# An opening in a pinned order: the short chunk's bias first, its stores and first reads ahead of loads of V, later K and weights

## The chip, the cores and the metric

The kernel runs on one core of one Trainium2 chip, as one program. The core has TensorE (PE in the profile), VectorE (DVE), ScalarE (ACT), GpSimd (POOL) and SyncE (SP, which here only issues transfers), and 16 DMA engines that move data between HBM and on-chip memory. The metric is the time of one execution in device microseconds, the median of several runs.

## The reference

Attention for 4 batch rows, 8 heads, 576 positions and head size 64, with a bias that a small network computes from the distance of two positions, followed by a feed-forward layer with a squared ReLU over 2304 tokens. Cut to what is computed:

```python
scores = (1 / sqrt(D)) * q @ k.T                       # 4 x 8 x 576 x 576
x = log1p(abs(i - j)) / log1p(max(i, 1))               # 576 x 576
bias = relu(x[..., None] @ w1 + b1) @ w2               # hidden size 32, one bias per head
attn = softmax(scores + bias); y = attn @ v            # 2304 x 512 after heads are joined
out = relu(y @ w_in) ** 2 @ w_out                      # 512 -> 2048 -> 512
```

## The kernel before

**Work.** The batch rows are taken in two pairs p, and each pair in five chunks c of queries: chunk 0 is the short one (the last 64 positions of both rows of the pair, in one tile of 128 rows), chunks 1 to 4 are 128 positions. A step is one (p, c, head); there are 80 steps, chunk by chunk in the order of ORDER, chunk 0 of pair 0 first. In a step, `qk` (L359) makes the scores on PE, `softmax_a` (L386) adds the bias tile `bt` and takes the row maximum on DVE (L398, the instruction by which the start of a step is told below) and exponentiates on ACT, `softmax_b` transposes, and three steps later `pv` multiplies with V. When the eight heads of a chunk are done, `finish_x` passes the chunk to the expert layer, which is worked through in eight units of 256 hidden columns (`g1`, tile `hp`, L522; `g2`, L545) between the steps. Most operands are split into two fp16 parts, so each weight block of 512 KB that is loaded costs three DVE operations of 512 columns (`WT.split`, L206, L207, L209), an ACT cast and two POOL operations. The 32 blocks are loaded (`ld_dma`) through three buffers and split (`ld_split`) by a list W_AT, three, then two a step.

**Bias.** The bias depends on two positions and a head only. It is computed once, in 36 groups of 16 positions, of which the four groups 32 to 35 belong to the short chunk and come first. For each group `hgen` (L268) makes four tiles of the hidden layer, on ACT or DVE by a pattern (`PATS[HID[...]]`, where A is ACT and D is DVE: "AADD" makes two on each). `bias_mm` (L303) multiplies them with `w2s` on PE in two pieces per group (288 columns and the rest), each into a PSUM tile `bp`, evicts each piece (L332 on ACT, L334 on DVE) into a tile `be` and stores it to the table `biasd` in HBM (L337). The first piece of a group has two evictions on ACT, the second one on DVE. `bias_ld` (L341) reads the table back, skewed, into the tile `bt` that a step adds: two loads of 144 KB for the short chunk, three buffers. The first step's loads must wait for all eight stores of the short chunk.

**Order.** The program is written as below; a planner then gives each engine and each DMA queue one fixed order, from the order of the text and its own estimate of when each instruction becomes ready. All plain transfers here go through SP's queue, which issues in order: an issue that waits holds up those behind it. Because a load of V or K needs only a free buffer, the planner could put it ahead of a store that was not ready. K of step t is loaded to one of two staging buffers (L162) and split by POOL (`kv_split`); V has nine buffers.

The lines that set the opening before:

```python
    nc.sync.dma_start(out=tab_t, in_=tabs)
    nc.sync.dma_start(out=sm_t, in_=sm)
    kv_dma(0)
    ...
    while gi < bias_due(-1):
        hgen(groups[gi], ("hg", "a", "at", "s")[gi % 4])
        bias_mm(groups[gi], gi)
        gi += 1
```

Of the kernel before, what the change touches and what calls it, by code (L numbers as in the profile page):

```python
# [2 lines left out]

# [5 lines left out]
F32 = mybir.dt.float32  # L9
# [4 lines left out]
ALU = mybir.AluOpType  # L14
# [19 lines left out]
}  # L34

PATS = ["DDDD", "ADDD", "AADD"]
HID = "222222222211111000"

W_AT = [3, 2, 2, 2, 2, 2, 2, 2, 2, 2, 2, 2, 2, 2, 2, 1]
ORDER = [[0, 3, 2, 4, 1], [1, 0, 4, 2, 3]]  # L40
# [9 lines left out]
def tile_attention_moe(  # L50
# [217 lines left out]
    def hgen(G, pl=None):  # L268
        ts_ = []
        for t in range(4):  # L270
            n = 4 * G + t
            if t % 2 == 0:
                if pl == "a":
                    h2 = a_p.tile([128, 2304], F16, tag="a", name="hg").bitcast(F32)
                elif pl == "at":
                    h2 = at_p.tile([128, 20, 128], F16, tag="at", name="hg").rearrange("p k i -> p (k i)").bitcast(F32)
                elif pl == "s":
                    h2 = s_p.tile([128, 1152], F32, tag="w", name="hg")
                else:
                    h2 = hg_p.tile([128, 1152], F32, tag="w", name="hg")  # L280
            ht = h2[:, (t % 2) * S:(t % 2) * S + dlen(G)]
            if hg_pat(G)[t] == "A":
                nc.scalar.activation(out=ht, in_=tab_t[:, 0:dlen(G)], func=AF.Relu,
                                     bias=sm_t[:, 1:2], scale=scl[:, n:n + 1])
            else:
                nc.vector.tensor_scalar(ht, tab_t[:, 0:dlen(G)], scl[:, n:n + 1], nb1, op0=ALU.mult, op1=ALU.max)  # L286
            ts_.append(ht)
        hg[G] = ts_

    def hconst():  # L290
        cp = ps_h.tile([128, 512], F32, tag="h", name="cp")
        for t in range(4):
            nc.tensor.matmul(out=cp[32 * t:32 * t + 32, 0:2], lhsT=w2s, rhs=sm_t[:, 1:3],
                             start=True, stop=True, tile_position=(0, 32 * t))
        nc.vector.tensor_scalar(nb1, sm_t[:, 1:2], -1.0, None, op0=ALU.mult)

        for z in sorted({hg_z(G) for G in groups}):
            nc.vector.tensor_copy(hcst[:, z:z + 1], cp[:, 0:1])
            for t in range(4):
                if PATS[z][t] == "A":  # L300
                    nc.vector.memset(hcst[32 * t:32 * t + 32, z:z + 1], 0.0)

    def bias_mm(G, gi):  # L303
        ts_ = hg.pop(G)
        z = hg_z(G)
        D_ = dlen(G)
        F_, M_ = S - 16 * G, 16 * G + 16
        cuts = [0, D_] if D_ <= 512 else [0, 288, D_]
        for d0, d1 in zip(cuts[:-1], cuts[1:]):
            bp = ps_h.tile([128, 512], F32, tag="h", name="bp")  # L310
            for t in range(4):
                nc.tensor.matmul(out=bp[32 * t:32 * t + 32, 0:d1 - d0], lhsT=w2s,  # L312
                                 rhs=ts_[t][:, d0:d1],
                                 start=True, stop=True, tile_position=(0, 32 * t))

            parts = [(max(d0, 1), min(d1, M_), True), (d0, min(d1, F_), False)]
            parts = [x for x in parts if x[1] > x[0]]
            runs = [parts] if d0 == 0 and sum(e - a for a, e, _ in parts) <= 512 else [[x] for x in parts]
            for run in runs:
                nbe[0] += 1  # L320
                if nbe[0] <= 16 and nbe[0] % 2:

                    be = as_f32(g_p.tile([128, 2, 512], F16, tag="g", name="be"))
                else:
                    be = r_p.tile([128, 512], F32, tag="r", name="be")
                p0 = 0
                for a, e, rev in run:
                    o = be[:, p0:p0 + e - a]
                    o = o[:, ::-1] if rev else o
                    p0 += e - a  # L330
                    if (zn("er" if rev else "ev") == "A") if gi > 4 else nbe[0] % 2:
                        nc.scalar.activation(out=o, in_=bp[:, a - d0:e - d0], func=AF.Identity, bias=hcst[:, z:z + 1])  # L332
                    else:
                        nc.vector.tensor_scalar(o, bp[:, a - d0:e - d0], hcst[:, z:z + 1], None, op0=ALU.add)  # L334
                a, e, rev = run[0]
                c0 = S - e if rev else S - 1 + a
                nc.sync.dma_start(out=biasd[128 * G:128 * G + 128, c0:c0 + p0], in_=be[:, 0:p0])  # L337

    b_t = {}

    def bias_ld(p, c, h):  # L341
        t = bt_p.tile([128, S], F32, tag="bt", name="bt")
        def rows(i0, n):
            o = (i0 * H + h) * LB + S - 1 - i0
            x = H * LB - 1
            return bias_f[o:o + n * x].rearrange("(i x) -> i x", x=x)[:, 0:S]

        if c == 0:
            for b in range(2):
                nc.sync.dma_start(out=t[64 * b:64 * b + 64, :], in_=rows(512, 64))  # L350
        else:
            nc.sync.dma_start(out=t, in_=rows(128 * (c - 1), 128))
        b_t[p, c, h] = t


    st_ = {}
# [213 lines left out]
    def bias_due(t):  # L570
        if t < 0:
            return due[0]
        ahead = min(AHEAD, t + 1)
        k = (t + ahead) // H + 1
        if k >= NCK:
            return len(groups)
        f = (t + ahead) % H + 1
        return due[k - 1] + -(-(due[k] - due[k - 1]) * f // H)
# [28 lines left out]
    def ld_dma(q):  # L607
        if q:
            t = q.popleft()
            t.dma()  # L610
            pend.append(t)
# [7 lines left out]

    def kv_dma(h):  # L620
        if h < H:
            for w in "vk":
                kv[h, w] = KV(0, h, w)
                kv[h, w].dma()

    def kv_split(h):
        if h < H:
            for w in "vk":
                kv.pop((h, w)).split()

    def w_tasks(i):
        for _ in range(W_AT[i] if i < len(W_AT) else 0):
            ld_split()
            ld_dma(ws)
# [4 lines left out]
    def q_next():  # L639
        if qi[0] < len(qlist):  # L640
            q_dma(*qlist[qi[0]])
            qi[0] += 1
# [18 lines left out]
    nc.vector.memset(eps, 1.0e-9 * 2.0 ** ESC)  # L661
    nc.vector.memset(esc, ESC * LN2)
    nc.scalar.activation(out=nb1, in_=hcst[:, 0:1], func=AF.Exp)
    nc.sync.dma_start(out=tab_t, in_=tabs)
    nc.sync.dma_start(out=sm_t, in_=sm)
    kv_dma(0)
    q_next()
    q_next()
    ld_dma(ws)
    ld_dma(ws)  # L670
    kv_dma(1)
    ld_dma(ws)
    nc.vector.tensor_scalar(w2s, sm_t[:, 2:34], float(2 ** (QS + KS + 3)), None, op0=ALU.mult)
    nc.vector.tensor_scalar(scl, scl, sm_t[:, 0:1], None, op0=ALU.mult)
    hconst()
    gi = 0
    while gi < bias_due(-1):
        hgen(groups[gi], ("hg", "a", "at", "s")[gi % 4])
        bias_mm(groups[gi], gi)
        gi += 1  # L680
    hgen(groups[gi])
    kv_split(0)
    q_split(*qlist[0])
    with later(200):
        q_next()
    with later(200):
        w_tasks(0)
    for h in range(2):
        bias_ld(*steps[h])
    for t in range(NS + LAG):  # L690
        now[0] = t
        last = t - LAG
        if t < NS:
            p, c, h = steps[t]
            qk(p, c, h)
            softmax_a(p, c, h)
            if t + 2 < NS:
                bias_ld(*steps[t + 2])
            if h % 4 == 2 and t + 2 < NS:
                q_split(*qlist[(t + 2) // 4])  # L700
                q_next()
            if len(moe) > BACKLOG:
                moe_unit()
            softmax_b(p, c, h)
            if last < 0 or steps[last][2] != H - 1:
                moe_unit()
        if last >= 0:
            pv(*steps[last])
            if steps[last][2] == H - 1:
                finish_x(*steps[last][:2])  # L710
        if t >= NS:
            if steps[last][2] != H - 1:
                moe_unit()
            if len(moe) > BACKLOG:
                moe_unit()
            continue
        while gi < bias_due(t):
            bias_mm(groups[gi], gi)
            gi += 1
            if gi < len(groups):  # L720
                hgen(groups[gi])
        kv_split(t + 1)
        kv_dma(t + 2)
        w_tasks(t + 1)
        for _ in range(nls[t]):
            ld_split()
            ld_dma(loads2)
        if NF * H <= t < NF * H + H:
            v_split(0, t - NF * H, v32.pop(t - NF * H))
        if t == 31:  # L730
            ld_dma(loads2)
            ld_dma(loads2)
    while moe:
        moe_unit()
    while g2q:
# [44 lines left out]
```

## Time and profile before

| | |
|---|---|
| time, median of 3 runs | 688.13 us (687.62 to 689.01) |
| profiled execution, span from first to last instruction | 683.4 us |
| what lies around the span, to the median of the runs | 4.7 us |
| mean granted clock of PE | 0.948 |
| busy: PE, DVE, ACT, POOL | 92%, 60%, 57%, 53% of the span |
| DMA | 112.16 MB, mean 164 GB/s |

The profile is of one execution. Its own time is not given apart from the span, so the 4.7 us are the difference to the median of the other runs. Busy shares are means over the whole span, while the opening, the stretch in which weights are split, and the rest have different limits; they are read stretch by stretch. [...]

### The profile page before, as it was taken

What the parts mean: (1) busy time and instruction counts of PE and PEld (TensorE: products, weight loads), DVE (VectorE), ACT (ScalarE), POOL (GpSimd) and SP (SyncE); (2) the same over time, 40 slices, a digit from 0 to 9 for tenths busy, and PEclk for the clock granted to TensorE, in tenths of its full rate; (3) what the DMA queues carried; (4) which work ended last, traced back from release to release, by engine and by line L of the source; (5) the groups of instructions that cost most, each with busy time, mean ns of one, the idle gap of its engine ahead of it and who ended that gap; (6) DMA issues with size and microseconds to landing.
All of it is one profiled execution on the core that took longest, in us unless ns stands there. A gap on an engine that the chain in (4) does not pass through costs nothing.

```text
span 683.4 us, 15528 instructions
## 1 busy us (share of the span) xinstructions
PE 630.2 (92%) x6048; PEld 405.1 (59%) x6048; DVE 412.1 (60%) x815; ACT 386.9 (57%) x857; POOL 360.4 (53%) x375
## 2 busy tenths in 40 slices
PE   5076989899899999999999999999989999999997
PEld 1033546666455556666666676666656776676664
DVE  6458899999966694577757434436448455424120
ACT  6377786878776465665755643455566565521211
POOL 4733446578556346667766543545456564632221
PEclk9668765999999999999999999999999999999999
DMA  8967688667896777899997796457699888452000
GB/s 294 321 175 227 198 236 244 188 198 190 185 192 167 139 172 165 179 198 222 217 186 159 138 175 116 107 111 160 138 198 188 165 161 156 94 113 32 32 1 31
DMA packets 206568, 112.16 MB, mean 164 GB/s; under 512 B 167072, under 2 KB 183456, under 8 KB 206496
## 3 DMA queue, kind: packets, MB, share of 16 engines
q1 hardware_dynamic: 206496, 111.19, 70.7%
q8 instruction: 47, 0.77, 0.5%
q14 instruction: 25, 0.20, 0.1%
HBM read 55.44 MB, written 15.61 MB: 104 GB/s over the span
## 4 chain that ended last, share of the span: by engine, by line
PE 59%; DMA 8%; DVE 5%; ACT 3%; issue 2%; POOL 1%; SPq 0%; ACTq 0%; DVEq 0%; POOLq 0%
PE hp L522 23%; PE o L545 22%; PE pv L468 6%; DMA at<-a 5%; PE sc L382 4%; PE bp L312 2%; DVE hg L286 1%; DMA xt<-xh 1%; PE sc L376 1%; PE sc L370 1%; ACT a L123 1%; DVE s L398 1%; DMA bt<-biasd 1%; DVE r L530 1%; DVE v L139 1%
## 5 line engine op out<-in xcount | busy, mean ns | idle before, releaser
L522 PE MATMUL hp<-xt,winH 128*128 128x256 f16 (+1 forms) x1280 | 197.6, 264 | 3.7 <-DMA xt<-xh 3.2
L545 PE MATMUL o<-woutH,g 128*128 128x512 f16 x576 | 185.3, 381 | 1.6 <-POOL g L532 0.8
L522 PE MATMUL hp<-xt,winL 128*128 128x256 f16 (+1 forms) x640 | 163.3, 264 | 0.0
L522 PEld LDWEIGHTS <-winH 128*128 128x128 f16 x1280 | 117.3, 99 | 39.1 <-issue 19.3
L545 PEld LDWEIGHTS <-g 128*128 128x128 f16 x864 | 83.1, 98 | 92.9 <-issue 7.7
L530 DVE TENSOR_TENSOR r<-hp,r 128x512 f32<-128x512 f32 (+1 forms) x80 | 50.7, 634 | 133.7 <-ACT r L528 129.6
L431 POOL TENSOR_TENSOR a<-s,a 128x1024 f16<-128x1024 f32 (+1 forms) x64 | 130.2, 2035 | 0.0
L532 POOL TENSOR_TENSOR g<-r,g 128x512 f16<-128x512 f32 (+1 forms) x80 | 86.3, 1079 | 77.7 <-DVE g L127 74.9
L398 DVE CUSTOM_DVE_ANT_0 s<-sc,bt 128x576 f32<-128x576 f32 x144 | 103.4, 750 | 38.2 <-PE sc L382 22.9
L404 ACT ACTIVATE s<-s,nm 128x576 f32<-128x576 f32 x144 | 111.4, 774 | 6.9
L545 PE MATMUL o<-woutL,g 128*128 128x512 f16 x288 | 109.4, 380 | 0.0
L402 ACT ACTIVATE nm<-mx,esc 128x1 f32<-128x1 f32 x144 | 41.3, 287 | 113.4 <-DVE mx L398 113.3
L430 POOL TENSOR_TENSOR a<-s,a 128x128 f16<-128x128 f32 (+1 forms) x64 | 28.4, 444 | 138.9 <-ACT a L123 129.0
L123 ACT ACTIVATE a<-s 128x1152 f16<-128x1152 f32 (+1 forms) x64 | 70.5, 1102 | 50.1 <-DMA at<-a 48.8
L528 ACT ACTIVATE r<-hp 128x512 f32<-128x512 f32 (+1 forms) x80 | 43.2, 540 | 60.6 <-PE hp L522 60.5
L468 PEld LDWEIGHTS <-at 128*128 128x128 f16 (+1 forms) x1792 | 60.3, 100 | 24.5 <-issue 7.6
L286 DVE TENSOR_SCALAR hg<-tab_t,nb 128x464 f32<-128x464 f32 (+17 forms) x94 | 61.7, 704 | 12.2 <-PE bp L312 12.1
L468 PE MATMUL pv<-v,at 128*128 128x64 f16 (+1 forms) x1792 | 64.1, 194 | 4.8 <-DMA at<-a 4.8
L522 PEld LDWEIGHTS <-winL 128*128 128x128 f16 x640 | 63.1, 99 | 6.4 <-issue 0.4
L382 PE MATMUL sc<-k,q 64*128 64x512 f16 x384 | 54.7, 391 | 0.0
L312 PE MATMUL bp<-hg,w2s 128*32 128x288 f32 (+17 forms) x352 | 46.1, 563 | 5.2 <-ACT at L417 1.8
L461 PEld LDWEIGHTS pv<-v,at 128*64 128x64 f32 (+3 forms) x320 | 39.0, 194 | 15.4 <-issue 10.3
(73 smaller groups left out, 683.4 us busy)
## 6 DMA issues: line engine op xcount, KB each, us to landing
bt<-biasd SPq DMA_DIRECT2D x64, 288.0 KB, 3.2
stg<-w_in SPq DMA_DIRECT2D x16, 512.0 KB, 4.6
stg<-w_out SPq DMA_DIRECT2D x16, 512.0 KB, 5.0
bt<-biasd SPq DMA_DIRECT2D x32, 144.0 KB, 3.6
qst<-qd SPq DMA_DIRECT2D x32, 128.0 KB, 3.4
out<-o SPq DMA_DIRECT2D x16, 256.0 KB, 2.4
v<-vd SPq DMA_DIRECT2D x8, 320.0 KB, 7.2
stg<-vd SPq DMA_DIRECT2D x8, 320.0 KB, 3.5
```

Source lines behind the costliest of these rows:

```text
L123: nc.scalar.activation(out=out, in_=in_, func=AF.Copy, scale=scale)
L286: nc.vector.tensor_scalar(ht, tab_t[:, 0:dlen(G)], scl[:, n:n + 1], nb1, op0=ALU.mult, op1=ALU.max)
L312: nc.tensor.matmul(out=bp[32 * t:32 * t + 32, 0:d1 - d0], lhsT=w2s, rhs=ts_[t][:, d0:d1], start=True, stop=True, tile_position=(0, 32 * t))
L382: nc.tensor.matmul(out=sc[:, 1024 * b:1024 * b + 512], lhsT=qt[r, qz, qs], rhs=kt[r, z, 64 * b:64 * b + 512], start=(n == 0), stop=(n == 2 ...
L398: nc.vector.tensor_tensor_reduce(s[:, 576 * b:576 * b + 576], sc[:, 960 * sb:960 * sb + 576], bt, inv, -3.0e38, ALU.add, ALU.max, mx[:, b: ...
L404: nc.scalar.activation(out=sl, in_=sl, func=AF.Exp, bias=nm[:, b:b + 1], accum_out=su[:, h, b:b + 1])
L431: nc.gpsimd.tensor_tensor(av[:, :, 640:1152], ev[:, :, 0:512], av[:, :, 0:512], op=ALU.subtract)
L468: nc.tensor.matmul(out=dst, lhsT=lhsT, rhs=vt[:, vz, 5 * b + blk, :], start=(n == 0), stop=(n == 13), tile_position=(0, 0 if c else 64 * b))
L522: nc.tensor.matmul(out=hp[:, f * T:f * T + T].rearrange("p (b t) -> p b t", b=nb), lhsT=wt[:, k, c0:c0 + 128], rhs=xt[:, 0:nb, z * 4 + k, ...
L530: nc.vector.tensor_tensor(rr, hp[:, 0:2 * T], rr, op=ALU.mult)
L532: nc.gpsimd.tensor_tensor(g[:, 1, 0:2 * T], r[:, 0:2 * T], g[:, 0, 0:2 * T], op=ALU.subtract)
L545: nc.tensor.matmul(out=blk["o"][b], lhsT=g[:, z, c0:c0 + 128], rhs=wt[:, 2 * u + f, :], start=(u == 0 and f == 0 and z == 0 and wt is wout ...
```

## The change

The opening is written anew. Everything from the first table load to the first two steps' bias loads stands in a block `pinned()`, in which each instruction follows the one before it on its engine (an order alone, without a wait): the small table before the large one, three weight blocks, one q tile and K of heads 0 and 1, then the four groups' tiles and pieces interleaved (tiles of group 1 before pieces of group 0, and so on), the eight stores, the split of K and q, two weight splits, the tiles of the fifth group, and the four bias loads. What follows, V of heads 0 and 1, K of head 2, more weight blocks and q, and all instructions of the first two steps, is put behind the last pinned instruction of its engine by `behind()`. For all heads, K is loaded before V, and both are issued after the last bias load written so far (`issue_after`). The second piece of each of the first four groups goes to a PSUM tile `o0` or `o1`, which the expert layer uses later, so that four PSUM tiles serve the pieces in place of two. HID begins with 1, so that groups 32 and 33 make one tile on ACT and three on DVE. The constant `nb1` is made on DVE before the first tiles.

```diff
--- before.py
+++ after.py
@@ -1,4 +1,4 @@
-from contextlib import ExitStack
+from contextlib import ExitStack, contextmanager
 from collections import deque
 
 import concourse.bass as bass
@@ -34,7 +34,7 @@
 }
 
 PATS = ["DDDD", "ADDD", "AADD"]
-HID = "222222222211111000"
+HID = "122222222211111000"
 
 W_AT = [3, 2, 2, 2, 2, 2, 2, 2, 2, 2, 2, 2, 2, 2, 2, 1]
 ORDER = [[0, 3, 2, 4, 1], [1, 0, 4, 2, 3]]
@@ -292,8 +292,6 @@
         for t in range(4):
             nc.tensor.matmul(out=cp[32 * t:32 * t + 32, 0:2], lhsT=w2s, rhs=sm_t[:, 1:3],
                              start=True, stop=True, tile_position=(0, 32 * t))
-        nc.vector.tensor_scalar(nb1, sm_t[:, 1:2], -1.0, None, op0=ALU.mult)
-
         for z in sorted({hg_z(G) for G in groups}):
             nc.vector.tensor_copy(hcst[:, z:z + 1], cp[:, 0:1])
             for t in range(4):
@@ -307,7 +305,10 @@
         F_, M_ = S - 16 * G, 16 * G + 16
         cuts = [0, D_] if D_ <= 512 else [0, 288, D_]
         for d0, d1 in zip(cuts[:-1], cuts[1:]):
-            bp = ps_h.tile([128, 512], F32, tag="h", name="bp")
+            if gi < 4 and d0:
+                bp = ps_o.tile([128, 512], F32, tag=f"o{gi % 2}", name="bp")
+            else:
+                bp = ps_h.tile([128, 512], F32, tag="h", name="bp")
             for t in range(4):
                 nc.tensor.matmul(out=bp[32 * t:32 * t + 32, 0:d1 - d0], lhsT=w2s,
                                  rhs=ts_[t][:, d0:d1],
@@ -337,6 +338,7 @@
                 nc.sync.dma_start(out=biasd[128 * G:128 * G + 128, c0:c0 + p0], in_=be[:, 0:p0])
 
     b_t = {}
+    bt_last = [None]
 
     def bias_ld(p, c, h):
         t = bt_p.tile([128, S], F32, tag="bt", name="bt")
@@ -347,10 +349,11 @@
 
         if c == 0:
             for b in range(2):
-                nc.sync.dma_start(out=t[64 * b:64 * b + 64, :], in_=rows(512, 64))
+                last = nc.sync.dma_start(out=t[64 * b:64 * b + 64, :], in_=rows(512, 64))
         else:
-            nc.sync.dma_start(out=t, in_=rows(128 * (c - 1), 128))
+            last = nc.sync.dma_start(out=t, in_=rows(128 * (c - 1), 128))
         b_t[p, c, h] = t
+        bt_last[0] = last.ins
 
 
     st_ = {}
@@ -619,14 +622,20 @@
 
     def kv_dma(h):
         if h < H:
-            for w in "vk":
-                kv[h, w] = KV(0, h, w)
-                kv[h, w].dma()
+            with tc.issue_after(bt_last[0]):
+                for w in "kv":
+                    kv_load(h, w)
+
+    def kv_load(h, w):
+        if (h, w) not in kv:
+            kv[h, w] = KV(0, h, w)
+            kv[h, w].dma()
 
     def kv_split(h):
         if h < H:
             for w in "vk":
-                kv.pop((h, w)).split()
+                if (h, w) in kv:
+                    kv.pop((h, w)).split()
 
     def w_tasks(i):
         for _ in range(W_AT[i] if i < len(W_AT) else 0):
@@ -661,34 +670,74 @@
     nc.vector.memset(eps, 1.0e-9 * 2.0 ** ESC)
     nc.vector.memset(esc, ESC * LN2)
     nc.scalar.activation(out=nb1, in_=hcst[:, 0:1], func=AF.Exp)
-    nc.sync.dma_start(out=tab_t, in_=tabs)
-    nc.sync.dma_start(out=sm_t, in_=sm)
-    kv_dma(0)
-    q_next()
-    q_next()
-    ld_dma(ws)
-    ld_dma(ws)
-    kv_dma(1)
-    ld_dma(ws)
-    nc.vector.tensor_scalar(w2s, sm_t[:, 2:34], float(2 ** (QS + KS + 3)), None, op0=ALU.mult)
-    nc.vector.tensor_scalar(scl, scl, sm_t[:, 0:1], None, op0=ALU.mult)
-    hconst()
-    gi = 0
-    while gi < bias_due(-1):
-        hgen(groups[gi], ("hg", "a", "at", "s")[gi % 4])
-        bias_mm(groups[gi], gi)
-        gi += 1
-    hgen(groups[gi])
-    kv_split(0)
-    q_split(*qlist[0])
-    with later(200):
+    @contextmanager
+    def pinned():
+        cur = nc.cur_bb
+        n0 = len(cur.bb.instructions)
+        yield
+        for i in cur.bb.instructions[n0:]:
+            prev = pin.get(i.engine)
+            if prev is not None:
+                tc.add_manual_dep(i, prev, mybir.DependencyInfo(
+                    mybir.DependencyClass.NoSync, mybir.DependencyReason.DATA), reason="pinned")
+            pin[i.engine] = i.name
+
+    @contextmanager
+    def behind():
+        cur = nc.cur_bb
+        n0 = len(cur.bb.instructions)
+        yield
+        for i in cur.bb.instructions[n0:]:
+            if i.engine in pin:
+                tc.add_manual_dep(i, pin[i.engine], mybir.DependencyInfo(
+                    mybir.DependencyClass.NoSync, mybir.DependencyReason.DATA), reason="behind")
+
+    pin = {}
+    with pinned():
+        nc.sync.dma_start(out=sm_t, in_=sm)
+        nc.sync.dma_start(out=tab_t, in_=tabs)
+        ld_dma(ws)
+        ld_dma(ws)
         q_next()
-    with later(200):
-        w_tasks(0)
-    for h in range(2):
-        bias_ld(*steps[h])
+        kv_load(0, "k")
+        ld_dma(ws)
+        kv_load(1, "k")
+        nc.vector.tensor_scalar(w2s, sm_t[:, 2:34], float(2 ** (QS + KS + 3)), None, op0=ALU.mult)
+        nc.vector.tensor_scalar(scl, scl, sm_t[:, 0:1], None, op0=ALU.mult)
+        nc.vector.tensor_scalar(nb1, sm_t[:, 1:2], -1.0, None, op0=ALU.mult)
+        hgen(groups[0], "hg")
+        hconst()
+        hgen(groups[1], "a")
+        bias_mm(groups[0], 0)
+        hgen(groups[2], "at")
+        bias_mm(groups[1], 1)
+        hgen(groups[3], "s")
+        bias_mm(groups[2], 2)
+        bias_mm(groups[3], 3)
+        kv_split(0)
+        q_split(*qlist[0])
+        ld_split()
+        ld_split()
+        gi = 4
+        hgen(groups[gi])
+        for h in range(2):
+            bias_ld(*steps[h])
+    with behind():
+        kv_load(0, "v")
+        ld_dma(ws)
+        kv_load(2, "k")
+        q_next()
+        kv_load(1, "v")
+        with later(200):
+            ld_split()
+            ld_dma(ws)
+            ld_dma(ws)
+            q_next()
     for t in range(NS + LAG):
         now[0] = t
+        fence = ExitStack()
+        if t < 2:
+            fence.enter_context(behind())
         last = t - LAG
         if t < NS:
             p, c, h = steps[t]
@@ -730,6 +779,7 @@
         if t == 31:
             ld_dma(loads2)
             ld_dma(loads2)
+        fence.close()
     while moe:
         moe_unit()
     while g2q:
```

## Rows read from the trace of the kernel before

**Rows 1.** The page: parts 1 and 2.

```profile
span 683.4 us, 15528 instructions
...
PE 630.2 (92%) x6048; PEld 405.1 (59%) x6048; DVE 412.1 (60%) x815; ACT 386.9 (57%) x857; POOL 360.4 (53%) x375
...
PE   5076989899899999999999999999989999999997
...
```

**Rows 2.** Busy time by stretch, in us: five engines, granted clock (share of full), DMA share, GB/s.

```profile
...
10.00:20.00 10.00, 6.75 (x52) 1.87 (x51) 6.64 (x15) 5.55 (x16) 5.62 (x10) 1.00 1.05 368
20.00:30.00 10.00, 0.00 (x0) 0.00 (x0) 6.14 (x9) 3.23 (x8) 8.70 (x11) 0.57 1.05 337
...
35.10:70.00 34.90, 25.82 (x191) 13.70 (x192) 25.06 (x46) 27.23 (x65) 12.73 (x14) 0.79 0.65 191
70.00:100.00 30.00, 26.86 (x191) 15.70 (x193) 26.03 (x51) 22.72 (x55) 14.93 (x17) 0.73 0.74 228
90.00:120.00 30.00, 29.31 (x137) 18.32 (x130) 28.11 (x48) 21.10 (x48) 17.97 (x21) 0.50 0.81 231
100.00:170.00 70.00, 66.87 (x530) 46.00 (x526) 67.05 (x123) 54.17 (x126) 48.75 (x62) 0.85 0.73 205
170.00:683.00 513.00, 500.20 (x5070) 326.43 (x5069) 274.40 (x557) 265.98 (x579) 262.69 (x252) 0.99 0.70 143
...
```

**Rows 3.** Tile hp on PE, 60 to 220 us: ns min/median/max, first and last start.

```profile
...
L522 PE MATMUL hp<-xt,winH x192: 216/219/421, 127.9 to 216.0; 128*128 128x128 f16 x128, 128*128 128x256 f16 x64
...
```

**Rows 4.** Order of time, PE: start, duration, instruction, idle before and its releaser.

```profile
...
13.33 5.45 PE L312 MATMUL bp<-hg,w2s 128*32 128x288 f32 x48 [1.37 <-DVE be L334]
35.91 1.62 PE L370 MATMUL sc<-k,q 128*128 128x64 f16 x6 [17.13 <-DVE mx L398]
...
```

**Rows 5.** Order of time, DVE, from 0 to 70 us.

```profile
...
4.67 1.49 DVE L286 TENSOR_SCALAR hg<-tab_t,nb 128x528 f32<-128x528 f32 x3
...
15.92 0.83 DVE L139 SCALAR_TENSOR_TENSOR v<-v 128x640 f16<-128x640 f32 x1
...
18.89 0.52 DVE L334 TENSOR_SCALAR be<-bp,hcst 128x288 f32<-128x288 f32 x1 [0.90 <-PE bp L312]
...
28.00 0.69 DVE L206 TENSOR_SCALAR ci<-stg 128x512 uint32<-128x512 uint32 x1 [2.44 <-DMA stg<-w_out]
...
35.09 0.76 DVE L398 CUSTOM_DVE_ANT_0 s<-sc,bt 128x576 f32<-128x576 f32 x1 [5.66 <-DMA bt<-biasd]
...
56.05 0.75 DVE L398 CUSTOM_DVE_ANT_0 s<-sc,bt 128x576 f32<-128x576 f32 x1
...
65.76 0.75 DVE L398 CUSTOM_DVE_ANT_0 s<-sc,bt 128x576 f32<-128x576 f32 x1
...
```

**Rows 6.** Order of time, SP: DMA issues from 0 to 70 us.

```profile
...
7.44 2.46 SPq L162 DMA_DIRECT2D v<-vd  x3
...
21.78 0.40 SPq L337 DMA_DIRECT2D biasd<-be  x1
...
26.14 4.57 SPq L350 DMA_DIRECT2D bt<-biasd  x6
...
```

**Rows 7.** DMA issues of 26 to 27.3 us: count, KB each, us to landing.

```profile
...
bt<-biasd SPq DMA_DIRECT2D x2, 144.0 KB, 8.2
```

**Rows 8.** DMA issues of 35.8 to 42.5 us.

```profile
...
bt<-biasd SPq DMA_DIRECT2D x6, 144.0 KB, 3.0
```

**Rows 9.** Order of time, ACT, from 0 to 70 us.

```profile
...
4.60 7.11 ACT L283 ACTIVATE hg<-tab_t,sm_t 128x528 f32<-128x528 f32 x10 [2.32 <-DVE tab_t L674]
...
12.24 0.70 ACT L332 ACTIVATE be<-bp,hcst 128x287 f32<-128x287 f32 x2
...
```

**Rows 10.** DVE by line and shape, 0 to 35 us: busy, mean ns.

```profile
...
L286 DVE TENSOR_SCALAR hg<-tab_t,nb 128x576 f32<-128x576 f32 x2 | 2.3, 1190 | 0.0
...
L286 DVE TENSOR_SCALAR hg<-tab_t,nb 128x544 f32<-128x544 f32 x2 | 1.1, 557 | 0.0
...
```

**Rows 11.** DMA issues of 42.5 to 47 us.

```profile
...
biasd<-be SPq DMA_DIRECT2D x1, 160.0 KB, 2.7
...
```

## The prediction

> **What bounds the kernel now.** I read the page first: its busy shares put TensorE (PE) far ahead, and its slices show where that is not so, namely in the first few [rows 1]. Then the busy times by stretch [rows 2]. From 170 us to the end PE is busy 500.20 of 513 us at a granted clock of 0.99: there the kernel is a fixed amount of PE work, and an earlier start of that stretch is an earlier end. From 100 to 170 VectorE (DVE) is busy 67.05 of 70 us, and in 70 to 100 26.03 of 30: the steps advance at DVE's pace there, mostly weight splits, and the first expert matmul starts only at 127.9 us [rows 3]. Before 70 neither holds: DVE idles 34.9 - 25.06 = 9.8 us of 35.1 to 70, and in 20 to 30 us PE does nothing at all while the DMA engines run at 337 GB/s with a share of 1.05.
>
> The order in time on PE shows what the opening waits for: the last bias piece ends at 18.78 us, and the next matmul comes at 35.91, after 17.13 us of idleness that ended with DVE's first row maximum [rows 4]. On DVE that first softmax (call it s0) starts at 35.09 and waited 5.66 us for the bias load [rows 5]. SyncE's (SP's) issues say why: the last of the eight bias stores is issued at 21.78, the loads that read them at 26.14 [rows 6], and the first two take 8.2 us to land [rows 7], where loads of the same size take 3.0 us in 35.8 to 42.5 [rows 8]. Between and before them stand loads of V, K and weights, three of V alone in one run at 7.44 [rows 6]. So a chain on its own, tables to bias to store to load, sets s0, and it runs through a queue filled with data that is wanted much later.
>
> **The pinned chain, part by part.** The two table loads swap and the large one is issued second; I add 0.2 us, so the hidden tiles start near 4.85 instead of 4.67 [rows 5]. From there DVE has ten tiles before the stores (three of groups 32 and 33 each, two of 34 and 35), at 1.49 / 3 = 0.5 us, four evictions of some 0.52, [rows 5], and the constants, for which I allow 0.4: 7.5 us if nothing waited. PE needs eight pieces at 5.45 / 6 = 0.91 us [rows 4]. ACT has six tiles (7.11 / 10 = 0.71 each) and four pairs of evictions of 0.70, 7.1 us [rows 9]. DVE, the longest, cannot end before 12.3. Followed group by group, with each engine in the pinned order: tiles of 32 done at 6.3, its pieces at 8.0, group 33's tiles at 8.5, 34's at 10.5, 35's at 12.0, its second piece on PE at 14.0, its eviction at 14.5. That includes about 1.3 us for tiles that run while GpSimd (POOL) splits K and q: the two tiles of 576 columns took 1190 ns on average, those of 544 columns 557 [rows 10].
>
> [...] Were all four late DVE tiles slowed like the slowest two, the chain would end some 1.2 us later than I take it.
>
> The second PSUM home for each group's later piece lets PE run both pieces of a group without waiting for an eviction; before, PE waited 1.37 us for one [rows 4]. That is already in the 14.5. The first score matmuls now stand behind all bias pieces on PE; six of them took 1.62 us at the low clock [rows 4], so they are done by 16 and hidden by the DMA round trip.
>
> Then the round trip. The last store is issued near 14.6. With SP pinned, nothing but tables, three weight blocks, q and two K tiles (2.7 MB, 8.0 us at 337 GB/s, landed by about 10) is ahead of it, so I take the quiet durations: 2.7 us for a store [rows 11], 0.5 for the second of two issues, 3.0 for a load [rows 8]. s0 comes at 20.8, and 35.1 - 20.8 is **14.3 us earlier**. Bounds: at the busy price of the load, 8.2 [rows 7], s0 comes at 26; with store and load each 1 us under the quiet rows, at 19.
>
> [...]
>
> **What is paid back.** By s0 DVE had also done, before: five more of the weight-split operations than the six that are pinned (eleven in all), at 0.69 [rows 5], a second q split of the same size and a V remainder of 0.83: 3.45 + 0.69 + 0.83 = 5.0 us. These now fall after s0, into the stretches where DVE sets the pace. The first digit of HID moves one tile of each of the first two groups from ACT to DVE: 2 x 0.55 = 1.1 us more on DVE in the early chain, already in the 14.5 at which the chain ends, and 1.4 off ACT; no work after s0 changes by it. Against the 5.0 stand 9.8 us of DVE idleness between s0 and 70 [rows 2], most of it in the first steps while results travel from engine to engine. I take 2.5 of the 5.0 as absorbed there (between 0 and 5.0).
>
> Next the DMA queue. Deferred past s0, by the tiles' shapes: eight V tiles (320 KB), five K tiles (288), three weight blocks (512), 384 KB of q, together 5,920 KB or 6.06 MB; at 337 GB/s 18.0 us of transfer. What is free: 35 percent of 34.9 us and 26 percent of 30 [rows 2], 20.0 us. It fits by a hair, on a queue that is nearly full for 65 us, and V is not wanted until three steps after its bias. But K for step t+2 now stands on SP behind the bias load of step t+2, which waits for a softmax to free one of three buffers; behind that waiting load stand weight loads, q, stores and DMA transposes too. Late K or late weight blocks cost DVE time in the early steps. No row shows this; it is bounded by nothing below and by some 9 us above (half of the 18.0). I take 3.
>
> Everything else in the diff (the constant's move, the fenced first two steps, K before V) I cost at nothing: the constant is one column on DVE, within the 0.4 allowed above, and the fences bind work that could not have run before s0 anyway, apart from the loads counted above. Without that cover the price is the 18.0 us.
>
> **Sum.** 14.3 - 5.0 + 2.5 - 3.0 = 8.8, rounded to 9 us, at the end of the DVE-paced stretch; PE's fixed work then passes it on. Profiled span 683.4 - 9 = 674.4. The page gives no time around its span; the median of the runs is 688.1, 4.7 above it, so **679.1 us**. About 0.2 percent, 1.4 us, is what a measurement of this kernel can tell from no change.
>
> **The rivals.**
> *The DMA queue takes it back.* The 18.0 us of deferred transfers do not fit the gaps, because SP stands in order behind waiting bias loads and the queue cannot use them. For it: share 1.05 at 368 and 337 GB/s in 10 to 30 us [rows 2], and some 3.4 us of queue time left empty between 10 and 17 us by the pin itself (7 us, less eight stores of about 150 KB). Against it: a step takes 9.7 us there (56.05 to 65.76, [rows 5]) and needs K, V, bias, two weight blocks and two stores, about 2.2 MB or 6.5 us. Cost 5 to 9 us in place of 3: gain 3 to 6, 682 to 685.
> *The whole shift arrives.* The 5.0 us are absorbed by the 9.8 and loads are never late: gain 14, 674.
> *Nothing arrives.* DVE's pace after s0 is set by chains between engines, whose order the planner draws anew, and its new order loses what the opening wins: 688.
> *Slower: TensorE's clock.* In 90 to 120 us PE was busy 29.31 of 30 us at a granted clock of 0.50 [rows 2]; that stretch ended just before the first expert matmul at 127.9 [rows 3], so it hit PE work while DVE was the pace. The clock fell after the gaps of the early steps. [...] It decides against the change once more than 18 us of half clock fall past the first expert matmul (half of which is the 9). Against it: from 170 us on the mean clock is 0.99.
>
> **How the numbers follow.** Forecast (gain 7 to 12, 676 to 681) 0.48; queue takes it back 0.22; whole shift 0.11; nothing 0.08; slower 0.11, in which I count a planner's order that loses outright. The range reaches from the whole shift to the queue's end, 673.5 to 685.5, and leaves out 0.19. Faster by over 0.2 percent 0.81, within 0.08, slower 0.11.
>
> **What would show it.** Right: s0 near 21 us in the order of time on DVE; the last bias store near 14.6 and its loads landing in about 3 us; PE's long idle stretch down from 17 to some 5 us; first expert matmul near 119; 170 to the end as full as before. Wrong: s0 early but DVE waiting for K, weight or V loads in 25 to 70 us; DVE's idle sum between s0 and the first expert matmul grown by more than the shift; or half clock past the first expert matmul.

## The result: 1.0 percent faster, 681.1 us

| | before | after |
|---|---|---|
| median (12 executions each) | 688.45 us (685.28 to 691.77) | 681.1 us (677.49 to 686.6) |
| ratio, 95% interval | | 0.9896 [0.9869, 0.9922] |
| profiled execution: span, granted clock | 683.4 us, 0.948 | 679.5 us, 0.964 |

The change is faster by 7.35 us, and 681.1 lies in the range forecast. Here and below, ratios leave out executions more than 1.5 percent above the fastest of the same kernel, medians keep them. The two profiled executions differ by only 3.9 us of span: of after, the profiled execution took 681.23 us, 1.7 more than its span and at the median; of before it was an execution some 3 us faster than its median (683.4 + 1.7 = 685.1). What follows compares these two, and says where that matters.

### The profile page after: what moved, and what is told of

Same layout as the page of the kernel before. It is cut to its first block, busy times and chain, and to the rows that moved or that the text cites. A ratio compares the mean times of both kernels' runs of the same rounds, so it can differ in the third digit from the quotient of the medians.

```text
span 679.5 us, 15519 instructions
## 1 busy us (share of the span) xinstructions
PE 626.5 (92%) x6048; PEld 404.7 (60%) x6048; DVE 413.2 (61%) x817; ACT 385.5 (57%) x855; POOL 362.8 (53%) x375
## 4 chain that ended last, share of the span: by engine, by line
PE 62%; DMA 15%; DVE 10%; ACT 6%; issue 4%; POOL 2%; SPq 1%; DVEq 0%; ACTq 0%; POOLq 0%
PE hp L525 21%; PE o L548 21%; DMA at<-a 7%; PE pv L471 6%; PE sc L385 4%; PE bp L313 4%; PE pv L464 2%; DVE hg L286 2%; DMA biasd<-be 2%; DMA kst<-kd 2%; DMA xt<-xh 2%; DVE s L401 2%; DMA bt<-biasd 1%; PE sc L373 1%; DMA stg<-w_in 1%
## 5 line engine op out<-in xcount | busy, mean ns | idle before, releaser
L123 ACT ACTIVATE a<-s 128x1152 f16<-128x1152 f32 (+1 forms) x64 | 70.5, 1102 | 42.3 <-DMA at<-a 41.1
L286 DVE TENSOR_SCALAR hg<-tab_t,nb 128x528 f32<-128x528 f32 (+17 forms) x96 | 63.2, 706 | 11.4 <-PE bp L313 11.1
L313 PE MATMUL bp<-hg,w2s 128*32 128x288 f32 (+17 forms) x352 | 48.9, 543 | 9.8 <-ACT at L420 3.4
L464 PEld LDWEIGHTS pv<-v,at 128*64 128x64 f32 (+3 forms) x320 | 36.8, 186 | 14.7 <-issue 11.3
(73 smaller groups left out, 679.5 us busy)
```

What stands on the lines that cost most here:

```text
L123: nc.scalar.activation(out=out, in_=in_, func=AF.Copy, scale=scale)
```

## The profile after

The page, parts 1, 2 and 4; it answers to [rows 1]:

```profile
span 679.5 us, 15519 instructions
...
PE 626.5 (92%) x6048; PEld 404.7 (60%) x6048; DVE 413.2 (61%) x817; ACT 385.5 (57%) x855; POOL 362.8 (53%) x375
...
PE   5578679889899999999999999999988999999997
...
PE 62%; DMA 15%; DVE 10%; ACT 6%; issue 4%; POOL 2%; SPq 1%; DVEq 0%; ACTq 0%; POOLq 0%
```

PE's slice that held 0 before (the second of 40) holds 5 now. The opening in order of time on DVE (answers to [rows 5]), SP (to [rows 6]) and PE (to [rows 4]):

```profile
4.75 1.49 DVE L286 TENSOR_SCALAR hg<-tab_t,nb 128x528 f32<-128x528 f32 x3
...
10.47 2.31 DVE L286 TENSOR_SCALAR hg<-tab_t,nb 128x576 f32<-128x576 f32 x2
...
14.03 0.52 DVE L335 TENSOR_SCALAR be<-bp,hcst 128x288 f32<-128x288 f32 x1 [0.85 <-PE bp L313]
...
19.30 1.05 DVE L286 TENSOR_SCALAR hg<-tab_t,nb 128x320 f32<-128x320 f32 x2
20.27 0.75 DVE L401 CUSTOM_DVE_ANT_0 s<-sc,bt 128x576 f32<-128x576 f32 x1
...
28.46 1.75 DVE L250 SCALAR_TENSOR_TENSOR q<-qst,q 128x512 f16<-128x512 f32 x1 [2.13 <-POOL q L125]
30.14 1.97 DVE L286 TENSOR_SCALAR hg<-tab_t,nb 128x304 f32<-128x304 f32 x2
...
32.48 0.74 DVE L401 CUSTOM_DVE_ANT_0 s<-sc,bt 128x576 f32<-128x576 f32 x1
...
48.49 0.83 DVE L286 TENSOR_SCALAR hg<-tab_t,nb 128x352 f32<-128x352 f32 x2
...
79.92 0.76 DVE L401 CUSTOM_DVE_ANT_0 s<-sc,bt 128x576 f32<-128x576 f32 x1 [3.17 <-DMA bt<-biasd]
```

```profile
8.22 6.81 SPq L338 DMA_DIRECT2D biasd<-be  x8
16.47 2.40 SPq L352 DMA_DIRECT2D bt<-biasd  x4
```

```profile
5.56 8.43 PE L313 MATMUL bp<-hg,w2s 128*32 128x288 f32 x64 [2.33 <-ACT hg L283]
...
22.30 1.11 PE L419 MATMUL tp<-ident,s 128*128 128x128 f32 x4 [6.68 <-ACT s L407]
```

The eight stores leave in one run with nothing between them, the last at about 14.65; the loads follow at 16.47, and the first softmax s0 stands at 20.27 instead of 35.09. The DMA issues of 14 to 16, of 16 to 19 and of 19 to 23 us (answers to [rows 7, 8, 11]):

```profile
biasd<-be SPq DMA_DIRECT2D x1, 144.0 KB, 1.8
...
bt<-biasd SPq DMA_DIRECT2D x4, 144.0 KB, 2.9
...
bt<-biasd SPq DMA_DIRECT2D x2, 144.0 KB, 5.8
```

On the emptied queue the store took 1.8 us and the first loads 2.9; four microseconds later, with V and weights on the queue, loads of the same size took 5.8. The second load that s0 needs, issued at 17.00, landed at 19.82, so the round trip took 5.2 us from the last store's issue. DVE's row for s0 shows no wait: two hidden tiles of the fifth group, pinned ahead of it, fill DVE up to it, and the last 0.4 us before s0 are theirs and not the load's.

Then the lead shrinks. Busy time of before, split at s0 (35.09) and at the start of step 18 (168.28), the last step at which the difference between the two kernels still moves; under it the same stretches of after (20.27 and 163.46), and then, for the stretch from s0 to step 18 of before and of after, DVE's operations on V alone (one V remainder for each V tile). Columns as in [rows 2]:

```profile
0.00:35.09 35.09, 10.40 (x78) 3.30 (x78) 19.55 (x42) 16.76 (x35) 21.25 (x32) 0.80 0.97 305
...
35.09:168.28 133.19, 117.84 (x876) 73.86 (x877) 116.43 (x213) 102.95 (x242) 74.70 (x90) 0.81 0.70 206
168.28:683.40 515.12, 501.92 (x5095) 327.98 (x5095) 276.12 (x562) 267.15 (x581) 264.41 (x254) 0.99 0.70 144
```

```profile
0.00:20.27 20.27, 9.45 (x78) 4.40 (x78) 15.52 (x37) 10.54 (x21) 5.92 (x14) 0.99 0.69 220
...
20.27:163.46 143.19, 115.16 (x874) 71.81 (x875) 122.74 (x222) 107.44 (x254) 93.16 (x109) 0.86 0.82 237
163.46:679.50 516.04, 501.92 (x5098) 328.51 (x5097) 274.91 (x562) 267.52 (x582) 263.73 (x253) 0.99 0.69 143
```

```profile
35.09:168.28 133.19, 7.73 (x7) 0.81 0.70 206
...
20.27:163.46 143.19, 9.97 (x8) 0.86 0.82 237
```

From step 18 on the two are equally long to 0.9 us: PE busy 501.92 us in both, 515.1 and 516.0 long. So nearly all is decided before step 18. s0 comes 14.8 us earlier; the stretch from s0 to step 18 is 10.0 us longer. DVE's column says of what: 116.43 us busy before, 122.74 after, 6.3 more, and 133.19 - 116.43 = 16.76 us idle before, 143.19 - 122.74 = 20.45 after, 3.7 more. Of the 6.3, 4.95 is work that before had done ahead of s0: five weight-split operations, a q split and a V remainder. (DVE's columns ahead of s0 differ by only 19.55 - 15.52 = 4.0, since two more hidden tiles run there now.) The other 1.4 is the same work taking longer; V remainders took 1.25 us on average instead of 1.10.

Where it is lost, by the starts of steps (row maxima on DVE) of the two kernels: s0 -14.8, s1 -5.1, s4 -8.9, s6 -9.8, s8 -4.5, s11 -9.0, s14 -6.9, s16 -4.9, s18 -4.8, and the same to the end within 0.9. The 9.7 us between s0 and s1 are explained by POOL's order of time and by the chain of waits, and experiment 2 tests it:

```profile
22.76 0.67 POOL L125 TENSOR_SCALAR k<-kst 128x576 f16<-128x576 f32 x1
25.92 0.67 POOL L125 TENSOR_SCALAR k<-kst 128x576 f16<-128x576 f32 x1 [2.49 <-DMA kst<-kd]
26.56 1.28 POOL L172 TENSOR_TENSOR k<-kst,k 128x576 f16<-128x576 f32 x1
27.80 0.62 POOL L125 TENSOR_SCALAR q<-qst 128x512 f16<-128x512 f32 x1
28.39 1.28 POOL L172 TENSOR_TENSOR k<-kst,k 128x576 f16<-128x576 f32 x1
29.75 0.94 POOL L125 TENSOR_SCALAR cv<-cv 128x512 f32<-128x512 f32 x1
```

```profile
20.02 5.83 DMA kst<-kd
25.92 0.62 POOL k L125
...
28.78 8.60 DMA stg<-w_in
...
38.61 5.39 DMA kst<-kd
...
70.08 5.78 DMA biasd<-be
75.94 3.84 DMA bt<-biasd
```

K of head 1 was on the chip early, and POOL cast it at 22.76; but POOL's next instruction is the cast of head 2's K, whose load was issued at 20.02 behind the bias loads and took 5.8 us, and only then come the subtractions. DVE then had a q split, which waited 2.13 us for POOL, two hidden tiles and an eviction ahead of s1. Of the page's chain, DMA's share rose from 8 to 15 percent. The second loss, from s6 to s8, is the first step of the next chunk: its bias, too, goes out to HBM and back (5.78 + 3.84 us), and DVE waited 3.17 us for it. Both losses are in part made good within a few steps. The 4.1 us lost between s11 and s16 stay lost: there DVE works 42.8 us instead of 40.4 and idles 1.7 us more.

The slower work is, as far as the rows show, DVE beside POOL. Two hidden tiles of 304 columns took 1.97 us at 30.14, while POOL cast and subtracted (29.75 to 31.93), and two of 352 columns 0.83 at 48.49, where POOL was idle (48.24 to 49.25). The two tiles of 576 columns took 1190 ns each in before [rows 10] and 2.31 us together here, both times while POOL split K and q (7.21 to 10.10 there, 9.64 to 12.47 here). Why it is slower there is not shown. Not every DVE operation is slowed: the weight-split operations up to step 18 took 0.67 to 0.72 us in both kernels, beside POOL or alone.

## The experiments

Medians; ratios are to the kernel before on the same chip. "Step n" is the start of that step in the profiled execution against before's first profile.

**1. The queue order alone, and the engines' order alone.** In the first, the two context managers act on SP's instructions only; in the second on all but SP's, and K and V are not put behind bias loads.

```diff
         for i in cur.bb.instructions[n0:]:
+            if i.engine != mybir.EngineType.SP:
+                continue
```

> Only SP's order is pinned, the other engines are left to the planner. Queue theory (most of the 14.8 us by which the first softmax moved come from what stands ahead of the bias loads on SP): stores end near 19 to 22 us as before the change, the bias loads land in about 3 us, the first softmax starts at 23 to 27, and the time lies at 681 to 685. Rival (the pinned order of the compute engines made the gain): first softmax near 33 to 35, time 687 to 689.

```diff
         for i in cur.bb.instructions[n0:]:
+            if i.engine == mybir.EngineType.SP:
+                continue
...
-            with tc.issue_after(bt_last[0]):
-                for w in "kv":
-                    kv_load(h, w)
+            for w in "kv":
+                kv_load(h, w)
```

> The compute engines are pinned, SP's queue is left to the planner and K and V are not held behind bias loads. Queue theory: the last bias eviction still ends near 14.5 us, but loads of V, K and weights get ahead of the bias loads again, which take 6 to 8 us; first softmax at 25 to 31, time 683 to 687. Rival (compute order): first softmax at 20 to 23 and time 680 to 682, as with the whole change.

Measured: SP alone 686.64 us, 0.996 [0.9929, 0.9992]; the engines alone 683.82, 0.9932 [0.9904, 0.996]. SP's order of time, of the first and of the second kernel:

```profile
10.94 6.73 SPq L338 DMA_DIRECT2D biasd<-be  x8
19.10 2.40 SPq L352 DMA_DIRECT2D bt<-biasd  x4
```

```profile
8.77 0.36 SPq L338 DMA_DIRECT2D biasd<-be  x1
9.17 0.92 SPq L162 DMA_DIRECT2D v<-vd  x2
...
16.43 1.55 SPq L338 DMA_DIRECT2D biasd<-be  x3
...
22.10 3.68 SPq L352 DMA_DIRECT2D bt<-biasd  x6
```

With SP's order alone s0 stands at 22.8, 12.3 earlier; with the engines' alone V gets between the stores again, the loads go out at 22.10, and s0 is at 27.9, 7.2 earlier. So for s0 the queue is the larger half and the engines' order adds 2.5 us. But neither lead lives: at step 8 they are 1.4 and 2.4 us ahead, at step 12 3.4 and 6.0, at step 13 nothing, and at step 18 0.3 and 0.2 (against a second profile of before, in experiment 3, 2.0 and 1.9). The medians go the other way: SP's order alone gains 2.0 us, less than the queue theory had it, the engines' alone 4.8. How early s0 is does not tell what arrives.

**2. K of head 1 split early**, which removes the loss at s1.

```diff
         kv_split(0)
         q_split(*qlist[0])
+        kv_split(1)
         ld_split()
```

> The split of K for the second step is pinned ahead of the two weight splits. The second softmax, which came only at 32.5 us in the changed kernel, should start at 22 to 25. DVE-balance theory (the end follows DVE's idle time and work up to the expert phase, not the start of single steps): DVE waited 4.0 us between 22 and 29 us, so at most that much is won, time 678 to 681. Rival (steps theory: the 9.7 us that the second step lost against the first are what is missing at the end): time 672 to 676.

Measured: 684.08 us, 0.9936 [0.9911, 0.9962], so slower than the change. s1 moved from 32.5 to 22.9 as meant, and step 4 was 12.2 us ahead; step 8 5.9, step 12 6.9, steps 14 to 21 1.1. Both theories missed. Busy time of this kernel in 100 to 120 us and from step 12 to 14, then of after from step 12 to 14; below, PE's order of time in this kernel and in after (12 matmuls of `pv`, and the same a step later):

```profile
100.00:120.00 20.00, 20.00 (x92) 13.11 (x92) 17.47 (x31) 13.67 (x33) 12.76 (x15) 0.50 0.73 220
...
114.60:134.90 20.30, 20.30 (x124) 14.60 (x124) 14.02 (x30) 13.82 (x34) 9.24 (x14) 0.63 0.46 133
```

```profile
113.06:129.10 16.04, 14.08 (x115) 10.08 (x115) 14.93 (x29) 13.22 (x31) 10.32 (x15) 0.89 0.70 203
```

```profile
107.53 3.20 PE L464 MATMUL pv<-v,at 64*128 64x64 f32 x12
...
118.00 3.20 PE L464 MATMUL pv<-v,at 64*128 64x64 f32 x12
```

```profile
114.36 1.83 PE L464 MATMUL pv<-v,at 64*128 64x64 f32 x12
...
121.02 1.83 PE L464 MATMUL pv<-v,at 64*128 64x64 f32 x12
```

At a granted clock of 0.50 PE is busy 20.00 of 20 us, and the same matmuls come round after 10.5 us (12 of them take 3.20 us), in after, at a granted clock of 1.00, after 6.7 (they take 1.83). From step 12 to 14 PE is busy 20.30 of 20.30 us while DVE does 14.02 us of work; in after DVE does 14.93 of 16.04. In this kernel DVE's waits there are 4.2 us for PE and 2.0 for POOL. So PE at a low clock, not DVE, set most of the pace of this kernel there, and it took 4.3 us longer for two steps: most of the 5.8 us of lead that went.

Experiment 1's kernels lost their leads in the same place. From step 12 to 13, of before, of SP's order alone and of the engines' alone:

```profile
121.50:127.64 6.14, 5.27 (x43) 3.90 (x40) 6.07 (x15) 5.33 (x13) 2.83 (x5) 1.00 0.58 160
```

```profile
118.10:127.66 9.56, 9.21 (x43) 5.77 (x43) 6.66 (x14) 6.27 (x16) 4.64 (x8) 0.50 0.65 177
```

```profile
115.53:127.59 12.06, 12.06 (x58) 8.66 (x58) 7.78 (x15) 7.29 (x18) 6.20 (x9) 0.50 0.55 154
```

At 1.00 DVE sets the pace of this step (busy 6.07 of 6.14 us); at 0.50 it is busy 6.66 of 9.56 and 7.78 of 12.06 us, and PE nearly throughout. A long stretch of low clock alone does not cost this: the kernel with HID as before (experiment 6) had one of 34.1 us from 79.5 to 113.6, but its step 12 to 13 ran at 1.00, took 6.7 us, and it kept its gain. The orders differ (the engines alone have 58 matmuls in this step, before 43), so this is a comparison and not a proof. Whether a lead holds without the low clock is the next question.

**3. Before again, and the clock held.** The first is the kernel before itself, once more; in the others the score matmuls of steps 8 to 15 are issued twice with the same result (nothing is left out), in the change, in experiment 2's kernel and in before, so that PE has more to do there. In after, the score matmuls of one such step took 0.34 and 0.82 us from 116.12, at a granted clock of 1.00; from these I estimate some 9 us more PE work in the eight steps.

```diff
-            for n, (qz, z) in enumerate(terms):
+            twice = terms * 2 if 8 <= now[0] < 16 else terms
+            for n, (qz, z) in enumerate(twice):
+                n = n % 3
```

> The kernel before, unchanged, for a second profile and as a null. Its profiled span of 683.4 us was 3.5 under the median span of its other runs. Clock theory: the second profile again has a stretch of half clock of 20 us or more between 85 and 135 us, and the steps after it shift with its length. Rival (the long stretch was chance): the stretch is absent and the span the same within 1 us. Ratio 1.000 within its interval.

The change with doubled matmuls:

> [...] Clock theory (an early lead is lost where PE runs at half clock between 85 and 135 us): if the added fp16 matmuls hold the clock, half clock falls under 7 us there, the steps from 13 on stand 2 to 4 us earlier, time 677 to 680. Rivals: PE work is the limit there and 9 us more of it shows, 686 to 690; or DVE alone sets the pace and nothing changes, 680 to 682.

> The kernel with the second step's K split pinned early, which led by 12 us at step 4 and lost it in 41 us of half clock, with the score matmuls of steps 8 to 15 issued twice. Clock theory: the stretch of half clock shrinks to under 15 us and the lead of 6 to 8 us at step 12 survives: time 675 to 680, against 684.1 without. Rival (PE work or DVE): 684 to 692.

> The kernel before with the score matmuls of steps 8 to 15 issued twice. Clock theory: its 30.7 us of half clock shrink, and the time falls by 2 to 6 us to 683 to 687 without any change of the opening. Rival: DVE was busy 95 percent in that stretch, so a faster PE gains nothing, and the added work costs 0 to 9 us: 688 to 697.

Measured: before again 688.5, 1.0007 [0.9972, 1.0041]; the change with doubled matmuls 681.54, 0.9916 [0.9879, 0.9953]; experiment 2's kernel with them 689.41, 1.0006 [0.9973, 1.0038]; before with them 692.35, 1.0048 [1.0013, 1.0083]. Busy time of 90 to 120 us in before again, and of 70 to 157.3 us, up to step 18, in the change with doubled matmuls:

```profile
90.00:120.00 30.00, 24.48 (x138) 14.18 (x139) 28.22 (x51) 20.87 (x50) 17.63 (x20) 0.68 0.80 231
```

```profile
70.00:157.30 87.30, 74.91 (x676) 49.14 (x674) 81.78 (x151) 66.75 (x158) 55.00 (x69) 1.00 0.75 213
```

In before again the mean clock of 90 to 120 is 0.68 instead of 0.50 [rows 2] and PE is busy 24.48 us instead of 29.31, yet DVE is busy 28.22 against 28.11 and the steps from 8 to 20 keep a constant distance of 1.7 us from the first profile. For before, then, the low clock cost nothing there; DVE was the pace. In the profiled execution of the change with doubled matmuls the clock stayed at 1.00 from 70 us to step 18, and step 18 came at 157.3, 6.2 us earlier than in the change. That execution (678.0 us) was the fastest of its twelve, the rest behind step 18 was 3 us longer, and the median did not move. Nor is the clock shown to be what won the 6.2 us: 3.8 of them were there at step 7 (66.6 us against 70.5), where the doubled matmuls begin, and only 2.4 came after that, so what a held clock is worth stays open. With experiment 2's kernel the doubling shortened the longest stretch of low clock up to step 18 from 41.0 to 10.2 us, but the time rose: step 18 came 1.5 us earlier than in before, and the rest behind it took 522.7 us, 6.4 more than in experiment 2. In before with doubled matmuls step 18 came 5.2 us later, and the rest took 520.7. Why the rest is longer, although the doubling ends before step 16, is not shown. Experiment 2's loss stays partly open.

**4. K and V not put behind the bias loads.**

```diff
-            with tc.issue_after(bt_last[0]):
-                for w in "kv":
-                    kv_load(h, w)
+            for w in "kv":
+                kv_load(h, w)
```

> K and V loads of later heads are no longer held behind the last bias load; the pinned opening stays. Queue-takes-it-back theory: late K behind waiting bias loads costs 3 to 6 us, so without it time 675 to 678. Rival (DVE balance): DVE's waits in 20 to 90 us are for weights, POOL, PE and bias, not for K, so time 680 to 682, within 1.5 us of the changed kernel; or slower, 683 to 686, if V comes ahead of weight blocks and bias again.

Measured: 680.12 us, 0.9881 [0.9854, 0.9908]; step 18 at 162.8, 0.7 earlier than in the change (the profiled execution is the fastest of six). The order that I had priced at 3 us costs some 1 by the medians, which these intervals cannot tell from nothing. It is the lowest median of all kernels that ran, but as a ratio no better than HID as before (experiment 6).

**5. Bias five groups ahead instead of three**, to take the wait at step 8 away; in the change, and with experiment 4's edit.

```diff
-AHEAD = 3
+AHEAD = 5
```

> The changed kernel with the later chunks' bias computed two steps earlier (AHEAD 5 in place of 3). Theory of the second round trip (the lead of 9.8 us at step 6 falls to 4.5 at step 8 because DVE waits 3.2 us for the first bias load of the next chunk): that wait goes, step 8 starts at 75 to 77 us instead of 79.9, and the end follows by 2 to 3 us, 678 to 679.5. Rival (DVE balance): the bias work only trades places with weight splits, the wait is filled or reappears elsewhere, step 18 stays within 1 us of 163.5 and the time within 680 to 682.

> As the last, with K and V also not held behind bias loads. Theory of the second round trip: 676 to 678.5. Rival: 679.5 to 681, as with free K and V alone.

Measured: 688.48, 0.9963 [0.9935, 0.9991], and 689.0, 0.9995 [0.9964, 1.0027]. The wait for `bt` at step 8 is gone from DVE's list, and step 8 comes at 85.0, 5.1 us later than in the change; DVE has done 144.2 us of work by step 18 instead of 138.3, and the rest behind it takes 519.2 us instead of 516.0. Both theories missed. Taking the wait away did not give its 3.2 us back: computing the bias earlier fills the DVE time before step 8 with other work, and more of it. With experiment 4's edit step 8 comes at 88.3 and step 18 at 174.7.

**6. The small parts: two PSUM tiles for the pieces, and HID as before.**

```diff
-            if gi < 4 and d0:
+            if False:
```

> The changed kernel with all bias pieces of the opening in the two PSUM tiles of before. If the four tiles matter, PE waits for evictions between the pieces and the last eviction ends 1 to 3 us after 14.5 us, the first softmax at 21.5 to 23.5. Rival (each piece is evicted before its tile is needed again): first softmax within 0.5 us of 20.3. The time at the end within 1.5 us of 681.1 by either.

```diff
-HID = "122222222211111000"
+HID = "222222222211111000"
```

> The changed kernel with HID as before, two hidden tiles on ACT and two on DVE in the first two groups. DVE has 1.1 us less and ACT 1.4 us more in the opening. If DVE is the longest chain there, the first softmax comes 0.3 to 1.0 us earlier; if ACT is, 0.3 to 1.4 us later. The time at the end within 1.5 us of 681.1 by either; by DVE balance up to 1 us better.

Measured: s0 at 20.3 and 20.2, as with the change: neither part is needed for the opening. HID as before gave 681.29 us, 0.988 [0.9853, 0.9908], no difference. With two PSUM tiles the twelve executions spread from 680.37 to 693.62, median 687.53, ratio 0.992 [0.9889, 0.9951]; the profiled one, with 690.82, is among the longer ones. Whether the PSUM tiles matter after s0 is open.

## Why the prediction was right, and where it was off

*The opening: right step by step.* Tiles from 4.75 (said 4.85), the last eviction at 14.03 + 0.52 = 14.55 (14.5), the load's landing 2.9 (3.0), s0 at 20.27 (20.8). The store took 1.8, not 2.7, so the round trip was 5.2 us instead of 6.2; but DVE's pinned tiles, and not the load, held s0 for the last 0.4 us, a limit that the forecast did not have. The two widest tiles, beside POOL, were slow as priced (2.31 us together, 2 x 1190 ns in before). PE's idle stretch fell from 17 to 6.7 us (some 5).

*The second PSUM home and HID:* I had counted the first into the chain as needed; it is not (experiment 6).

*What is paid back: the step that was mis-sized.* The deferred DVE work was 5.0 us, as forecast. But I let 2.5 of it be absorbed in DVE's idle time, and nothing was: idle time rose by 3.7 us, where 3.0 for the queue less 2.5 absorbed would have let it rise by 0.5. The queue's 3.0 comes near that rise in size, yet not in place: K and weights are late, as the chain shows, at s1 and after it, but undoing the K order gives some 1 us. And a term was missing, 1.4 us for the same DVE work taking longer. In the profiled pair 10.0 us of 14.8 were paid back, where I had 5.5 of 14.3. Against the second profile of before (s0 at 35.87, step 18 at 170.0) it is 9.0 of 15.6. Both profiles of before come from executions some 3 us below its median, so no trace here shows where the rest of the 7.35 us arises.

*The time around the span: the second error, of opposite sign.* I took 4.7 us from a profile and the median of other executions. It is 1.7; the other 3 were the profiled execution of before being a fast one. Its 29 other executions beside the first experiments have spans of 682.7 to 692.1, median 686.9. So the span of after was to be 674.4 and is 679.5, while the time was to be 679.1 and is 681.1. The span was 5.1 us too low and the time around it 3.0 too high, so that the sum missed by only 2 is in part luck. The gain of medians, 7.35 us, lies near the 9 forecast although the profiled pair gained 3.9, because the profiled before stands for 3 us less than the typical one.

*PE's fixed work passes it on: right for the change.* From step 18 to the end before takes 515.1, before again 514.2, the change 516.0, experiments 1, 2 and 4 514.4 to 516.3. It is not so in every order: the kernels with doubled matmuls take 518.9 to 522.7 from there, and the change with the bias five groups ahead 519.2. The first expert matmul starts at 118.9, as said (119), 9.0 us earlier; but 4 of these 9 us were lost after it, up to step 18, so that was the wrong mark to watch.

*The rivals.* The queue takes it back: its mechanism is on the chain, its price not (experiment 4). The whole shift: no. Nothing arrives: no, but part of its mechanism is there, since idle time on DVE grew instead of shrinking, and experiment 5's kernels with the same opening kept little or none of the gain. Slower by the clock: for before the clock decided nothing (before again), and in the change the stretches of low clock were short (the longest after s0 10.2 us, from 101.7 to 111.9); but one of 41 us, from 88.6 to 129.6, is in experiment 2's profile, where 5.8 us of lead went from step 12 to 14, and in experiment 1's leads of 3.4 and 6.0 us went from step 12 to 13 at 0.50. The rival had the mechanism right for other orders than the one that ran.

*Open:* what starts the long stretches of low clock, and how much of the losses in experiments 1, 2, 5 and 6 is theirs and how much the planner's, which draws the whole order anew with each edit.

## What to carry to other kernels

A chain through memory that sets the first step was priced well here from the rows of its links on a quiet queue (s0 said at 20.8, measured at 20.27), but its gain is not yet the kernel's: find the step from which the rest is a constant (here 18, and not in every order), and count the pacing engine's work and idle time up to there. The work that was pushed behind the chain came back at full price here, 5.0 us, and the same DVE work took 1.4 us longer, as far as the rows show where it ran beside POOL. Take the time around a span from an execution that has both numbers, and compare one profile with one profile only to within the spread of executions.

## What the runs showed of the hardware that was not expected

One program's clock differs between executions: before had a stretch at half clock of 30.7 us from 89.6 in one profile, and in the other 6.8 us from 90.4, 3.4 from 100.7 and 10.2 from 110.9. PE can stay at 0.50 while it is busy without a gap (20.00 of 20 us in experiment 2's kernel). And one program's executions spread by 9 us (677.49 to 686.6 for the change).
